# Zero-padded keys, later routing matmuls, a longer filler burst and an earlier gather in a two-stage attention and expert kernel

## The chip, the cores and the metric

The kernel runs on one core of one Trainium2 chip. The metric is the device time of one execution in microseconds (us); the median of three runs is what is compared. [...]

## What is computed

Four batches of eight-head causal attention (sequence 768, head size 64) are followed by a mixture of eight experts over the 3072 tokens. Heads 0, 2 and 6 see the whole causal triangle; the other five see the first four keys ("sinks") and a band of 64 keys.

```
scores = scale * q @ k.T            # per batch and head, causal, or band + 4 sinks
a = softmax(scores); x = a @ v      # 3072 tokens x 512
do_compute = x @ w_skip > 0         # the other tokens pass unchanged
e = argmax(x @ w_gate)              # one expert of eight for each token
out = x + prob_e * (relu(x @ w1[e]) @ w2[e])
```

## The kernel before

The order of all instructions is the order of the program text; each engine works its own instructions in that order and waits on semaphores for the others.

**Attention.** A loop over the four batches runs six slots each (`slots`, `for b in range(B)`). The heads go in pairs (0,2), (4,6), (1,3), (5,7). `trans` turns q and k of a pair on PE: 24 small transposes, of which 12 write the first head to PSUM partitions 0 to 63 and the second to 64 to 127. ACT copies the q half to the tile qT, DVE the k half to kT, so that a pair of heads shares one 128-partition tile. `retr` computes scores of a full head in three chunks (two of 1024 PSUM columns, one of 640): it writes the mask with `ident` times `tri`, adds keys times queries, and ACT takes the exponential. `strm` does a banded head in one go of 768 columns: the mask by `ident`, then six blocks, each split into two output halves of 64 keys. Both read only the 64 partitions of their own head (`r`), so these matmuls use 64 of the array's 128 rows. `sinks` does the four sink keys of the five banded heads with a 128-row, 20-column stationary operand. `outp` multiplies attention by values for a block of 128 queries of the batch before, `xt` transposes the result, `gates` computes the expert logits. PSUM holds two score buffers (`sp`) and two transposition buffers (`tp`, shared by `trans`, `xt` and routing).

**Loads.** q, k and v are converted to 16 bits by DMAs that POOL issues; `dma_step(b)` at a batch's end issues v of the next batch, q and k of the one after it, and one expert's weights. All go through one queue in order.

**Routing.** `route` is a generator, advanced by `go_on` once in each slot of the last batch and of the tail; it runs for half of the tokens at a time. PE's matmuls `rps` (ranks) and `tbp` (the slot table) stand between DVE steps. The second half runs behind the attention with bursts of `fills` between the steps: matmuls of `ident` with a zero tile, whose result is not used.

**Experts.** `gather` fetches the tokens of an expert, `xin` casts them on DVE, transposes them on PE and copies them on ACT; `up_` and `down` are the two matmul layers. For expert e the order is up_(e+1), xin(e+2), down(e).

## Time and profile before

| | us |
|---|---|
| median of 3 runs | 278.56 (278.28 to 280.26) |
| the profiled execution | 276.57 |
| its span, first to last instruction | 274.7 |
| PE busy, share of the span | 85% |
| DVE, ACT, POOL busy | 42%, 33%, 27% |
| mean granted PE clock | 0.70 |

The time of the profiled execution is 1.9 us above its span: that lies around the program. Times in the rows count from the first instruction. By place in the program: the first scores start at 9.15, the batches' first scores at 9.15, 35.29, 74.57 and 116.46; the attention outputs of the last batch run to 174.97 (the tail), the second half of the routing to 186.39, the experts to the end. PEclk is 0.50 over nearly all of the attention and 1.00 over the experts.

### The profile page before, as it was taken

What the parts mean: (1) busy time and instruction counts of PE and PEld (TensorE: products, weight loads), DVE (VectorE), ACT (ScalarE), POOL (GpSimd) and SP (SyncE); (2) the same over time, 40 slices, a digit from 0 to 9 for tenths busy, and PEclk for the clock granted to TensorE, in tenths of its full rate; (3) what the DMA queues carried; (4) which work ended last, traced back from release to release, by engine and by line L of the source; (5) the groups of instructions that cost most, each with busy time, mean ns of one, the idle gap of its engine ahead of it and who ended that gap; (6) DMA issues with size and microseconds to landing.
All of it is one profiled execution on the core that took longest, in us unless ns stands there. A gap on an engine that the chain in (4) does not pass through costs nothing.

```text
span 274.7 us, 5076 instructions
## 1 busy us (share of the span) xinstructions
PE 234.1 (85%) x2158; PEld 140.4 (51%) x2158; DVE 115.6 (42%) x282; ACT 90.9 (33%) x125; POOL 72.9 (27%) x86
## 2 busy tenths in 40 slices
PE   7799989999999999799999579792889888898930
PEld 2445545555555556455566457341666545564610
DVE  1734444244433335423458752572243334534420
ACT  2666554523254432354343134200332223122100
POOL 8652830000530000420000000006862525523540
PEclk9755575555555555755558955599599999999985
DMA  5999999999399971299511123103899999994110
GB/s 75 174 166 161 72 184 222 220 227 224 58 158 221 227 152 59 63 157 223 114 41 50 68 79 115 41 0 119 185 181 246 209 297 212 210 256 161 66 57 8
DMA packets 53137, 39.54 MB, mean 144 GB/s; under 512 B 27945, under 2 KB 44329, under 8 KB 53104
## 3 DMA queue, kind: packets, MB, share of 16 engines
q0 software_dynamic: 49648, 32.82, 79.6%
q1 hardware_dynamic: 3456, 6.29, 6.5%
q8 instruction: 19, 0.31, 0.4%
q14 instruction: 14, 0.11, 0.1%
HBM read 56.66 MB, written 10.49 MB: 244 GB/s over the span
## 4 chain that ended last, share of the span: by engine, by line
PE 69%; DVE 8%; DMA 8%; ACT 5%; issue 4%; POOL 3%; POOLq 0%; DVEq 0%; ACTq 0%
PE sps L303 10%; PE myp L654 9%; PE mhp L639 6%; DMA xg<-out_dram,idg 6%; PE sps L315 5%; PE av L359 4%; PE tps L390 4%; PE tps L265 4%; PE sps L319 3%; PE sps L300 3%; PE av L369 3%; ACT qT L274 2%; ACT atr L306 2%; PE sps L331 2%; PE sps L323 2%
## 5 line engine op out<-in xcount | busy, mean ns | idle before, releaser
L306 ACT ACTIVATE atr<-sps 128x1024 f16<-128x1024 f32 (+1 forms) x36 | 32.6, 916 | 44.2 <-PE sps L303 44.2
L601 POOL DMA_INDIRECT xg<-out_dram,idg x16 | 16.4, 1026 | 79.6 <-DVE gs L592 68.0
L303 PE MATMUL sps<-qT,kT 64*128 64x512 f16 (+3 forms) x96 | 31.6, 453 | 3.2 <-DVE kT L276 3.2
L105 POOL DMA_DIRECT2D va<-in_v_dram x8 | 11.3, 1424 | 74.3 <-PE tps L265 35.7
L639 PE MATMUL mhp<-mxT,w1t 128*128 128x256 f16 x256 | 30.6, 281 | 0.0
L654 PE MATMUL myp<-w2t,ht 128*128 128x512 f16 x128 | 28.8, 379 | 0.0
L639 PEld LDWEIGHTS <-w1t 128*128 128x128 f16 x256 | 25.8, 101 | 4.9
L276 DVE COPY kT<-tps 128x768 f16<-128x768 f16 x16 | 15.3, 955 | 27.2 <-PE tps L265 27.2
L374 DVE RECIPROCAL rec<-av 128x8 f32<-128x8 f32 x18 | 3.7, 208 | 52.9 <-PE av L371 52.9
L325 ACT ACTIVATE ats<-sps 128x768 f16<-128x768 f32 x20 | 16.2, 810 | 27.2 <-PE sps L323 27.2
L656 DVE SCALAR_TENSOR_TENSOR xg<-myp,gs,xg 128x512 f32<-128x512 f32 x16 | 12.0, 751 | 23.1 <-PE myp L654 22.2
L658 POOL DMA_INDIRECT out_dram<-xg,idx x16 | 15.9, 992 | 21.0 <-DMA w2t<-in_moe_w_dram 4.3
L645 ACT ACTIVATE ht<-mhp 128x512 f16<-128x512 f32 x16 | 9.6, 597 | 33.6 <-issue 21.8
L643 DVE TENSOR_SCALAR ht<-mhp 128x512 f16<-128x512 f32 x16 | 11.1, 692 | 19.4 <-PE mhp L639 19.4
L654 PEld LDWEIGHTS <-ht 128*128 128x128 f16 x128 | 12.3, 98 | 13.5
L628 ACT COPY mxT<-mtp 128x512 f16<-128x512 f16 x16 | 8.8, 588 | 28.0 <-PE mtp L626 28.0
L390 PE MATMUL tps<-ident,x 128*128 128x128 f16 x96 | 13.7, 293 | 4.8 <-ACT qT L274 3.7
L319 PEld LDWEIGHTS <-kT 64*64 64x64 f16 x120 | 11.6, 155 | 12.1 <-issue 11.5
L626 PE MATMUL mtp<-ident,mx 128*128 128x128 f16 x64 | 6.6, 238 | 12.8 <-DVE mx L623 12.8
L251 PE MATMUL sps<-fill,ident 128*128 128x512 f16 x52 | 15.5, 458 | 1.7 <-DVE ident L133 1.7
L323 PE MATMUL sps<-qT,kT 64*64 64x64 f16 (+2 forms) x140 | 16.3, 283 | 0.0
L319 PE MATMUL sps<-qT,kT 64*64 64x128 f16 x120 | 16.2, 300 | 0.0
(141 smaller groups left out, 389.8 us busy)
## 6 DMA issues: line engine op xcount, KB each, us to landing
w1t<-in_moe_w_dram POOLq DMA_DIRECT2D x8, 1024.0 KB, 16.8
w2t<-in_moe_w_dram POOLq DMA_DIRECT2D x8, 1024.0 KB, 20.4
out_dram<-x SPq DMA_DIRECT2D x24, 256.0 KB, 2.4
va<-in_v_dram POOLq DMA_DIRECT2D x8, 384.0 KB, 8.6
qin<-in_q_dram POOLq DMA_DIRECT2D x3, 768.0 KB, 15.1
kin<-in_k_dram POOLq DMA_DIRECT2D x3, 768.0 KB, 18.1
qin<-in_q_dram POOLq DMA_DIRECT2D x2, 192.0 KB, 4.9
kin<-in_k_dram POOLq DMA_DIRECT2D x2, 192.0 KB, 5.8
```

Source lines behind the costliest of these rows:

```text
L251: nc.tensor.matmul(ps[:, :512], ident, fill, start=True, stop=True)
L276: nc.vector.tensor_copy(o, i_)
L303: nc.tensor.matmul(ps[:, x:x + n], kT[b, pr][r, j * P:(j + 1) * P], qT[b, pr][r, q0:q0 + n], start=False, stop=True, skip_group_check=True)
L306: nc.scalar.activation(at[b, h][:, o:o + w], ps[:, :w], ACT.Exp, scale=SCALE)
L319: nc.tensor.matmul(ps[:D, c:c + P], kt[r, c:c + D], qt[r, c:c + P], start=False, stop=True, skip_group_check=True)
L323: nc.tensor.matmul(ps[D:, x:y], kt[r, c + D:c + P], qt[r, x:y], start=False, stop=True, skip_group_check=True)
L325: nc.scalar.activation(a, ps[:, :S], ACT.Exp, scale=SCALE)
L390: nc.tensor.matmul(ps[:, s], xs[g][:, s * P:(s + 1) * P], ident, is_transpose=True, start=(s == 0), stop=(s == DS - 1))
L601: nc.gpsimd.indirect_dma_start(out=xg[e, t], out_offset=None, in_=out[:, :], in_offset=bass.IndirectOffsetOnAxis(ap=idg[:, sl:sl + 1], axi ...
L639: nc.tensor.matmul(hp[:, u], w1t[:, s, f * P:(f + 1) * P], xT[:, s], start=(s == 0 and u == 0), stop=(s == DS - 1 and u == 1))
L654: nc.tensor.matmul(yp, hts[e][:, f, t * P:(t + 1) * P], w2t[:, f], start=(f == 0), stop=(f == FS - 1))
L658: sc = nc.gpsimd.indirect_dma_start(out=out[:, :], out_offset=bass.IndirectOffsetOnAxis(ap=idx[:, sl:sl + 1], axis=0), in_=xg[e, t], in_of ...
```

## The change

Every head gets a key tile of its own, `kz`, with 128 partitions: the head's keys in its own 64, zeros in the other 64. The zeros are written once, before the first batch. `trans` copies the two halves of the transposed keys apart: DVE both of them for the pairs 0 and 2, DVE the first and ACT the second for the pairs 1 and 3. `retr` and `strm` multiply all 128 partitions of `kz` by all 128 of qT. In `route`, a step ends behind the `rps` matmuls instead of behind the DVE work after them, and all twelve `tbp` matmuls come one step after the DVE work that feeds the second six. The first filler burst has 14 matmuls instead of 10, and 6 more follow the first transposes. Four experts' gathers instead of three are issued ahead of the fifth expert's weights, and xin(e+2) moves between the two token tiles of down(e).

```diff
+    kz = {h: ac.tile([P, S], FP16, name=f"kz{h}") for pr in PAIRS for h in pr}
+    for pr in PAIRS:
+        nc.vector.memset(kz[pr[0]][D:], 0.0)
+        nc.vector.memset(kz[pr[1]][:D], 0.0)
...
     def trans(b, pr):
-        for name, src, dst in (("qT", q_in, qT), ("kT", k_in, kT)):
+        for name, src in (("qT", q_in), ("kT", k_in)):
...
-            t = qtp.tile([P, S], FP16, tag=name, name=name)
-            dst[b, pr] = t
-            o = t.rearrange("c (p n) -> c p n", n=NT)
             i_ = ps.rearrange("c n p -> c p n")
             if name == "qT":
-                nc.scalar.copy(o, i_)
-            else:
-                nc.vector.tensor_copy(o, i_)
...
+                t = qtp.tile([P, S], FP16, tag=name, name=name)
+                qT[b, pr] = t
+                nc.scalar.copy(t.rearrange("c (p n) -> c p n", n=NT), i_)
+                continue
+            for i, h in enumerate(PAIRS[pr]):
+                r = slice(i * D, (i + 1) * D)
+                o = kz[h][r].rearrange("c (p n) -> c p n", n=NT)
+                if i and pr % 2:
+                    nc.scalar.copy(o, i_[r])
+                else:
+                    nc.vector.tensor_copy(o, i_[r])
...
     def retr(b, pr, i, c):
-            nc.tensor.matmul(ps[:, x:x + n], kT[b, pr][r, j * P:(j + 1) * P],
-                             qT[b, pr][r, q0:q0 + n], start=False, stop=True,
+            nc.tensor.matmul(ps[:, x:x + n], kz[h][:, j * P:(j + 1) * P],
+                             qT[b, pr][:, q0:q0 + n], start=False, stop=True,
...
     def strm(b, pr, i):
-            nc.tensor.matmul(ps[:D, c:c + P], kt[r, c:c + D], qt[r, c:c + P],
+            nc.tensor.matmul(ps[:D, c:c + P], kt[:, c:c + D], qt[:, c:c + P],
-                nc.tensor.matmul(ps[D:, x:y], kt[r, c + D:c + P], qt[r, x:y],
+                nc.tensor.matmul(ps[D:, x:y], kt[:, c + D:c + P], qt[:, x:y],
...
     def route(c0, n):
+        yield
 
         sm = mk("sm", [P, n])
...
-        yield
         rk = mk("rk", sh)
...
-            for i in range(h0, h0 + NT):
-                nc.tensor.matmul(tb, ol[:, i], mv[:, i], start=(i == 0), stop=(i == n - 1))
             yield
+            if h0:
+                for i in range(n):
+                    nc.tensor.matmul(tb, ol[:, i], mv[:, i], start=(i == 0),
+                                     stop=(i == n - 1))
...
-    fills(10)
+    fills(14)
     trans(0, 0)
+    fills(6)
...
-        for e in range(3):
+        for e in range(4):
             gather(e)
         load_w(NW, wp2)
-        for e in range(3, 5):
+        for e in range(4, 6):
...
         def down(e):
             for t in range(T2):
+                if t and e + 2 < E:
+                    xin(e + 2)
```

On DVE, behind the first batch's mask constants, the key copies of the pairs 1 and 2 stand so before (skq is the sink keys' tile, vraw a constant):

```order
L276 COPY kT<-tps 128x768
L280 COPY skq_116<-kT 64x4
L192 MEMSET vraw 20x260
L276 COPY kT<-tps 128x768
L280 COPY skq_116<-kT 64x4 x2
```

and so now:

```order
L286 COPY kz_110<-tps 64x768
L289 COPY skq_132<-kz_110 64x4
L197 MEMSET vraw 20x260
L286 COPY kz_112<-tps 64x768
L289 COPY skq_132<-kz_112 64x4
L286 COPY kz_113<-tps 64x768
L289 COPY skq_132<-kz_113 64x4
```

Pair 2 has a second copy of the same length on DVE; the second head of pair 1 is absent here because ACT copies it, between a qT copy and the next exponential.

On DVE in the expert stage, the casts of xin(2) (mx) and the updates of down(0) (xg) with the last relus (ht) stand so before:

```order
L643 TENSOR_SCALAR ht<-mhp 128x512 x4
L623 CAST mx_2800<-xg_0_2619 128x512
L623 CAST mx_2808<-xg_1_2623 128x512
L656 SCALAR_TENSOR_TENSOR xg_0_2603<-myp,gs,xg_0_2603 128x512
L656 SCALAR_TENSOR_TENSOR xg_1_2607<-myp,gs,xg_1_2607 128x512
```

and so now:

```order
L652 TENSOR_SCALAR ht<-mhp 128x512 x4
L667 SCALAR_TENSOR_TENSOR xg_0_2630<-myp,gs,xg_0_2630 128x512
L632 CAST mx_2840<-xg_0_2646 128x512
L632 CAST mx_2848<-xg_1_2650 128x512
L667 SCALAR_TENSOR_TENSOR xg_1_2634<-myp,gs,xg_1_2634 128x512
```

The casts moved from behind the last relu to behind the first update of down.

On PE the first routing's table matmuls (tbp) stood between a transposition of attention outputs (x) and the next outputs (avt, the tail's); now the tail's outputs follow the transposition, and tbp comes behind a later gate matmul.

## Rows read from the trace of the kernel before

**Rows 1.** By stretch: length, busy of PE, PEld, DVE, ACT, POOL, PEclk, DMA, GB/s

```profile
35.29:74.57 39.28, 37.93 (x386) 22.59 (x387) 16.02 (x36) 15.81 (x19) 3.71 (x4) 0.53 1.10 193
74.57:116.46 41.89, 38.98 (x403) 22.91 (x403) 16.89 (x38) 15.92 (x19) 6.22 (x7) 0.54 0.97 146
116.46:152.79 36.33, 35.27 (x386) 20.75 (x387) 18.34 (x54) 15.21 (x19) 1.91 (x3) 0.58 0.82 117
152.79:174.97 22.18, 16.00 (x215) 12.05 (x215) 10.24 (x23) 7.20 (x13) 0.00 (x0) 0.60 0.23 84
```

**Rows 2.** PE by stretch: length, busy (instructions), PEclk, DMA share, GB/s

```profile
24.91:31.04 6.13, 6.13 (x62) 0.50 0.63 47
31.04:34.31 3.27, 3.27 (x35) 0.50 2.14 137
34.31:37.70 3.39, 2.60 (x27) 1.00 2.29 156
174.97:177.67 2.70, 2.70 (x11) 0.50 0.00 0
177.67:181.00 3.33, 3.33 (x28) 1.00 0.00 0
```

**Rows 3.** Groups by form, PE, 24.91 to 31.04: busy us, mean ns

```profile
L319 PE MATMUL sps<-qT,kT 64*64 64x128 f16 x24 | 3.4, 308 | 0.0
```

**Rows 4.** Groups by form, PE, 31.04 to 34.31

```profile
L331 PE MATMUL sps<-qT,skq 128*20 128x512 f16 x3 | 1.5, 622 | 0.0
L265 PE MATMUL tps<-ident,qin 128*64 128x128 f16 x12 | 0.9, 315 | 0.0
```

**Rows 5.** Timeline of PE, third batch: start, length in us

```profile
75.54 0.39 PE L300 MATMUL sps<-tri,ident 128*128 128x128 f16 x2
...
76.83 0.27 PE L401 MATMUL av<-WgAll,xT 128*128 128x9 f16 x4
...
103.86 0.82 PE L315 MATMUL sps<-smask,ident 128*128 128x512 f16 x2
...
105.39 0.27 PE L401 MATMUL av<-WgAll,xT 128*128 128x9 f16 x4
...
107.60 0.61 PE L390 MATMUL tps<-ident,x 128*128 128x128 f16 x4
```

**Rows 6.** Timeline of PE, the same work at the upper clock

```profile
35.83 0.28 PE L300 MATMUL sps<-tri,ident 128*128 128x128 f16 x2
...
36.58 0.23 PE L359 MATMUL av<-va,atr 128*128 128x65 f16 x2
...
147.50 0.26 PE L401 MATMUL av<-WgAll,xT 128*128 128x9 f16 x4
...
149.03 0.40 PE L390 MATMUL tps<-ident,x 128*128 128x128 f16 x4
...
149.26 0.49 PE L315 MATMUL sps<-smask,ident 128*128 128x512 f16 x2
...
150.14 0.98 PE L331 MATMUL sps<-qT,skq 128*20 128x512 f16 x6
```

**Rows 7.** The tile kin, load issued at 33.9: instructions, time to landing

```profile
L100 POOL DMA_DIRECT2D kin<-in_k_dram x1: 923/923/923, 33.9 to 33.9; - x1
...
DMA to landing us min/median/max: 24.4/24.4/24.4
```

**Rows 8.** Groups by form, all: busy us, mean ns, idle before and releaser

```profile
L251 PE MATMUL sps<-fill,ident 128*128 128x512 f16 x52 | 15.5, 458 | 1.7 <-DVE ident L133 1.7
...
L276 DVE COPY kT<-tps 128x768 f16<-128x768 f16 x16 | 15.3, 955 | 27.2 <-PE tps L265 27.2
```

**Rows 9.** Timeline of PE around the first routing

```profile
155.91 0.35 PE L481 MATMUL tbp<-mv,ol 128*128 128x64 f16 x6 [2.83 <-DVE ol L477]
...
159.56 0.50 PE L481 MATMUL tbp<-mv,ol 128*128 128x64 f16 x6 [1.65 <-DVE ol L477]
```

**Rows 10.** Timeline of PE in the expert stage

```profile
222.45 0.73 PE L626 MATMUL mtp<-ident,mx 128*128 128x128 f16 x8 [1.12 <-DVE mx L623]
```

## The prediction

> **What bounds the kernel now.** I first split the span at the batches' first scores and read each stretch's engine times and PEclk [rows 1]. PE is the busy engine: 38.98 of the third batch's 41.89 us, with DVE at 16.89 and ACT at 15.92. Those two have room; PE does not. [...]

> [...] I cut short stretches at the places where the level changes [rows 2]. From 24.91 to 31.04 PE was busy all the time, and the clock stayed at 0.50. From 31.04 to 34.31 it was again busy all the time, and right after that the clock stood at 1.00 for 3.39 us. The stretches differ in the shapes. The first is made of matmuls on a quarter of the array, 64 rows by 64 columns [rows 3], with a mask matmul ahead of each head. The second has the sink scores, 128 rows by only 20 columns, and transposes that read 128 rows [rows 4]. Twenty columns raised the clock where 64 by 64 did not, so width is not the difference; the array rows that are fed are. The fillers show the same: they feed 128 rows, and the clock rose at 177.67 behind them, although their moving operand is all zeros [rows 2]. Zeros in half of the rows should therefore count like data.

> Against this reading: the sink scores of the second batch are followed by no rise, and its stretch stays at 0.53 [rows 1]. One such group is no guarantee; what stands around it matters too.

> **What the change does, part by part.**

> *Padded keys.* The score matmuls keep their number and their columns and feed 128 rows instead of 64. By the reading above they become work of the kind that raises the clock. What the upper level is worth is read from the same work at both. A 1024-column chunk of a full head, start of its masks to the start of what follows, took 76.83 - 75.54 = 1.29 us at the lower level [rows 5] and 36.58 - 35.83 = 0.75 at the upper [rows 6]. A banded head took 105.39 - 103.86 = 1.53 [rows 5] and 150.14 - 149.26 = 0.88 [rows 6]. Gates and outputs of the fifth block took 107.60 - 105.39 = 2.21 [rows 5] and 149.03 - 147.50 = 1.53 [rows 6], a ratio of 0.69.

> A batch has six long chunks, three short ones (896 of 1280 columns with the masks, so 0.70 of a long one: 0.90 and 0.53 us) and five banded heads: 6 x 1.29 + 3 x 0.90 + 5 x 1.53 = 18.1 us now and 6 x 0.75 + 3 x 0.53 + 5 x 0.88 = 10.5 at the upper level, a gain of 7.6. PE's other work in the third batch is 38.98 - 18.1 = 20.9 us; at the ratio of the outputs it gains 31%, 6.5 us. Together 14.1 us of a batch of 41.9 if the clock stayed up. PE would then take about 28 us, above ACT and DVE with what is added to them (below), so PE stays the longest.

> I do not expect it to stay up throughout. After the rise at 34.31 it lasted 3.39 us, and PE had a pause in it: 2.60 busy [rows 2]. Such pauses are at each batch's start, where the first scores wait for the key copy. I take about 4 us of each 28 at the lower level, so 85% up, and subtract what was up already, (PEclk - 0.5) / 0.5: 8% in the third batch, 16% in the fourth [rows 1]. Third batch: 14.1 x 0.77 = 10.9. Fourth: 14.1 x 0.69 = 9.7.

> The first two batches have another limit. The keys of the third were issued at 33.9 and landed 24.4 us later [rows 7], at 58.3, behind loads that keep the queue full; a faster PE does not move that. Twelve transposes and a copy of 0.96 [rows 8] put the third batch's first scores at 59.8 at the earliest, against 74.57. The first two batches gain at most 14.8 us. By PE alone they would gain 14.1 x 0.79 = 11.1 in the second and, by my estimate, a third to a half of that in the first, which has no outputs of an earlier batch and waits for the second batch's keys: 15 to 16. So the landing decides, narrowly: 14.8. Attention: 14.8 + 10.9 + 9.7 = 35.4 us.

> *Two half copies for one.* A copy runs over 768 elements per partition whichever partitions it has, so I take 0.955 us for each half [rows 8]: one more for each of 16 pairs, half of them on DVE and half on ACT. Per batch that is two each, 1.9 us on engines with 25 and 26 idle us of 41.9 and still 9 to 10 of 28. The first head's copy comes first, and its scores (0.75) run under the second one. A new wait comes with pair 3: the copy of sink keys on DVE waits for ACT's key copy, which stands behind exponentials; queued behind it on DVE is the copy of the transposed outputs, for which gates wait two slots later. I take 0. The bound, all on the path, is 16 x 0.955 = 15.3 us.

> [...]

> *Routing a step later.* The table matmuls stand in front of the tail's outputs and wait for DVE: PE idles 2.83 and 1.65 us [rows 9]. With the outputs moved ahead and the inputs a step earlier, both go: 4.5 us. What is late next is DVE, which has the same work, 18.34 of 36.33 us busy [rows 1]; bounds 0 and 4.5. In the second half, six more table matmuls come behind the last DVE work, 0.35 us for six [rows 9]: +0.4.

> *Fillers.* Ten more at 0.458 us each [rows 8] are at most 4.6 us at the start. The landing of the third batch's keys covers most of them, since the first two batches would have up to a microsecond to spare, and part of them lies under the wait for the first key copy. I take 0; the bound is 4.6.

> *Experts.* PE idles 1.12 us between up and the transposes of xin [rows 10], since the cast stands behind the last relu on DVE. Now the cast stands behind the first update of down, which itself waits for PE. The wait changes its partner, not its kind: 0, bounds -6.7 (six of them gone) and +1. The earlier gather changes the order of loads that land with time to spare: 0.

> **Sum.** 276.57 - 35.4 - 4.5 + 0.4 = 237.1 us for the profiled execution. The median of the runs is 2.0 above its own profiled one; I put the time between the two, at 238.

> **The rivals.**

> *A, the forecast.* [...] With the clock always up, 14.8 + 13.0 + 11.8 + 4.5 - 0.4 and some 3 us from a tail at the upper level: 230. Up half of the time: about 249. Own range 229 to 249.

> *B, the clock swings.* If transposes count for nothing, only the last three slots of a batch, the banded heads, are raised, and the slots with transposes fall back. Gain per batch 5 x 0.65 + 3 x 0.68 = 5.3, over three batches and the first one's heads (3.3): 19.2; 276.6 - 19.2 - 4.5 + 0.4 = 253, with the median's offset 255. For it: most slots hold 24 transposes. Against it: the 31.04 stretch is half transposes and was followed by a rise [rows 2, 4]. [...]

> *C, no change in the clock.* If what raised it were the sink scores as such, attention stays as it is: 276.6 - 4.5 + 0.4 + 2 for fillers, about 275, within 1%.

> *D, slower.* As C, and the half copies hold the transposition buffers so long that PE waits: +15.3, about 290. It decides once the waits of PE for kz and tps grow by more than 4.5 + 2.8 us. Against it: the idle time of DVE and ACT.

> **How the numbers follow.** A 0.70, B 0.19, C 0.06, D 0.05. Time 238, A's. The range reaches from A's lower end over B: 229 to 256. Faster by over 1% (about what a measurement tells from no change) is A, B and a little of C: 0.90; same 0.05; slower 0.05.

> **What would show it.** PEclk of the batches above 0.85; a long chunk at about 0.75 us in any batch; third batch's first scores near 60, held by the landing of kin; no PE idle ahead of tbp in the first routing; the pause ahead of xin still near 1.1. I am wrong if score stretches stay at 0.50 with 128 rows fed, if ACT or DVE ends PE's waits for most of a batch, or if loads of v hold the third and fourth batch.

## The result and the profile after

The changed kernel takes 241.12 us (median of four runs, 238.51 to 242.65) against 279.04 for the kernel before (four runs, 278.28 to 280.26). The ratio is 0.861 with a 95% interval of 0.852 to 0.869: faster by 14%. The profiled execution took 238.51 us, with a span of 236.6 and a mean granted clock of 0.90. Runs of one program differed by the clock that they were granted (of 32 runs of the kernel before beside the experiments below, four took 260 to 264 us at a mean clock of 0.77, a gain of 8% against those, and the others 273 to 281), so every time below is a median with its range.

PE is TensorE, and PEclk is the clock that it was granted, in parts of full speed. It was 0.50 from 98.33 to 111.26 us in the kernel before and 1.00 from 60.54 to 114.94 us in the changed one; these are the lower and the upper level. The granted clock of the changed kernel, in 40 slices of the span (tenths of full speed):

```profile
PEclk9998988999999999999955579659999999999975
```

It is up through the attention, low in the tail (slices 21 to 23), low once more at the start of the experts (slices 26 and 27), and up over the rest of them. By stretch, to be set beside [rows 1]; the columns are length, busy time of PE, PEld, DVE, ACT and POOL, PEclk, DMA share and GB/s:

```profile
9.33:31.81 22.48, 15.49 (x222) 9.86 (x220) 15.37 (x43) 16.90 (x21) 11.15 (x18) 0.92 1.66 149
31.81:60.54 28.73, 24.35 (x386) 16.88 (x387) 17.90 (x38) 17.20 (x21) 6.10 (x7) 0.94 1.41 217
60.54:89.00 28.46, 23.40 (x402) 16.56 (x403) 18.88 (x40) 17.31 (x21) 6.22 (x7) 1.00 1.47 219
89.00:114.94 25.94, 22.83 (x389) 16.19 (x390) 19.36 (x52) 16.57 (x21) 1.91 (x3) 1.00 1.43 217
114.94:134.74 19.80, 15.36 (x215) 11.61 (x213) 10.91 (x28) 7.20 (x13) 0.00 (x0) 0.60 0.28 102
134.74:147.73 12.99, 12.25 (x68) 5.25 (x65) 8.61 (x34) 0.28 (x1) 0.00 (x0) 0.82 0.00 0
147.73:236.60 88.87, 64.13 (x449) 42.16 (x449) 29.49 (x52) 18.34 (x32) 39.61 (x40) 0.90 0.79 171
```

The third batch went from 41.89 to 28.46 us with the same number of instructions on PE, whose busy time fell from 38.98 to 23.40. DVE and ACT have two more copies each, and take no longer than PE. The same work as in [rows 5], on PE in the third batch (start, length in us):

```profile
79.84 0.50 PE L321 MATMUL sps<-smask,ident 128*128 128x512 f16 x2
...
80.73 0.26 PE L407 MATMUL av<-WgAll,xT 128*128 128x9 f16 x4
...
82.26 0.40 PE L396 MATMUL tps<-ident,x 128*128 128x128 f16 x4
```

A banded head takes 80.73 - 79.84 = 0.89 us, gates and outputs 82.26 - 80.73 = 1.53: the lengths that [rows 6] had at the upper clock. PE's waits from the second batch to the tail (us, times, longest), before and then after:

```profile
PE tps L390 <- ACT qT L274: 3.7, 10, 0.6
PE sps L303 <- DVE kT L276: 2.4, 3, 1.2
...
PE tps L396 <- ACT qT L278: 8.5, 10, 1.0
PE sps L310 <- DVE kz L286: 4.6, 6, 1.6
```

PE now waits longer for the engines that clear its buffers: 13.1 us instead of 6.1.

### The profile page after: what moved, and what is told of

Read it like the earlier page. It is cut to its first block, busy times and chain, and to the rows that moved or that the text cites. A ratio compares the mean times of both kernels' runs of the same rounds, so it can differ in the third digit from the quotient of the medians.

```text
span 236.6 us, 5118 instructions
## 1 busy us (share of the span) xinstructions
PE 185.5 (78%) x2168; PEld 121.8 (51%) x2168; DVE 125.8 (53%) x298; ACT 96.1 (41%) x133; POOL 73.3 (31%) x86
## 2 busy tenths in 40 slices
DMA packets 53137, 39.54 MB, mean 167 GB/s; under 512 B 27945, under 2 KB 44329, under 8 KB 53104
## 4 chain that ended last, share of the span: by engine, by line
PE 55%; DVE 15%; DMA 13%; ACT 6%; issue 5%; POOL 2%; DVEq 0%; POOLq 0%; ACTq 0%
PE mhp L648 10%; PE myp L665 9%; DMA out_dram<-xg,idx 7%; PE sps L256 7%; DVE kz L286 4%; DMA vraw<-in_v_dram 4%; PE sps L310 4%; PE av L365 3%; PE tps L396 3%; PE av L375 3%; ACT qT L278 2%; PE sps L321 2%; DVE x L382 2%; PE mtp L635 2%; PE sps L325 2%
## 5 line engine op out<-in xcount | busy, mean ns | idle before, releaser
L665 PE MATMUL myp<-w2t,ht 128*128 128x512 f16 x128 | 29.8, 379 | 0.0
L286 DVE COPY kz<-tps 64x768 f16<-64x768 f16 x24 | 22.8, 951 | 9.6 <-PE tps L270 9.1
L105 POOL DMA_DIRECT2D va<-in_v_dram x8 | 11.3, 1423 | 47.9 <-PE av L377 22.6
L310 PE MATMUL sps<-qT,kz 128*128 128x512 f16 (+3 forms) x96 | 20.5, 320 | 4.6 <-DVE kz L286 4.6
L652 DVE TENSOR_SCALAR ht<-mhp 128x512 f16<-128x512 f32 x16 | 11.1, 691 | 20.9 <-PE mhp L648 19.8
L331 ACT ACTIVATE ats<-sps 128x768 f16<-128x768 f32 x20 | 16.2, 809 | 10.7 <-PE sps L329 10.1
L396 PE MATMUL tps<-ident,x 128*128 128x128 f16 x96 | 10.7, 241 | 12.4 <-ACT qT L278 8.5
L256 PE MATMUL sps<-fill,ident 128*128 128x512 f16 x62 | 18.9, 471 | 1.7 <-DVE ident L133 1.7
L278 ACT COPY qT<-tps 128x768 f16<-128x768 f16 x16 | 12.7, 794 | 8.3 <-PE tps L270 8.1
L307 PE MATMUL sps<-tri,ident 128*128 128x128 f16 x72 | 10.3, 227 | 5.0 <-ACT atr L313 5.0
L396 PEld LDWEIGHTS <-x 128*128 128x128 f16 x96 | 6.9, 105 | 13.9 <-issue 8.3
```

Of the source, the lines that this page charges most:

```text
L256: nc.tensor.matmul(ps[:, :512], ident, fill, start=True, stop=True)
L278: nc.scalar.copy(t.rearrange("c (p n) -> c p n", n=NT), i_)
L286: nc.vector.tensor_copy(o, i_[r])
L310: nc.tensor.matmul(ps[:, x:x + n], kz[h][:, j * P:(j + 1) * P], qT[b, pr][:, q0:q0 + n], start=False, stop=True, skip_group_check=True)
L331: nc.scalar.activation(a, ps[:, :S], ACT.Exp, scale=SCALE)
L396: nc.tensor.matmul(ps[:, s], xs[g][:, s * P:(s + 1) * P], ident, is_transpose=True, start=(s == 0), stop=(s == DS - 1))
```

## The experiments

The table gives the stretches of each profiled execution: from first scores to first scores for the batches, then to the end of the last gate matmul, of the last tbp, and of the span. The median over the runs of each kernel stands last.

| kernel | batch 1 | batch 2 | batch 3 | batch 4 and tail | 2nd routing | experts | median us (range) |
|---|---|---|---|---|---|---|---|
| before | 26.1 | 39.3 | 41.9 | 58.7 | 9.3 | 90.3 | 279.0 (278.3 to 280.3) |
| after | 22.5 | 28.7 | 28.5 | 45.7 | 11.0 | 90.9 | 241.1 (238.5 to 242.7) |
| half_rows | 26.2 | 39.5 | 40.8 | 56.3 | 11.0 | 90.7 | 275.4 (266.4 to 277.8) |
| full_only | 24.2 | 29.4 | 28.4 | 47.6 | 10.7 | 91.1 | 242.0 (239.6 to 244.2) |
| band_only | 26.2 | 37.6 | 38.2 | 53.9 | 11.3 | 91.0 | 270.6 (269.9 to 271.3) |
| pad_only | 23.0 | 29.3 | 28.5 | 50.9 | 10.1 | 91.5 | 245.6 (243.2 to 247.4) |
| seam | 21.6 | 28.5 | 26.4 | 45.3 | 11.2 | 88.8 | 232.9 (229.7 to 234.1) |
| six | 22.6 | 24.3 | 24.7 | 44.9 | 8.2 | 83.6 | 220.4 (218.7 to 222.6) |
| six_tail | 22.0 | 24.3 | 24.5 | 43.6 | 8.2 | 84.5 | 219.1 (218.5 to 221.1) |

The kernel before, run again beside them, took 278.0 us (with half_rows, full_only, band_only and pad_only), 279.3 (with fill_trans, vsk_late, vsk_loads and xin_early), 276.6 (with xt_first, seam and six) and 276.5 (with six_tail). The changed kernel was not run again beside them; its 241.1 is from its own four runs. The kept trace is of the longest run for vsk_late and xin_early, and of the shortest for the changed kernel and six.

**half_rows: is it the array rows?** All edits stay, and only the score matmuls go back to 64 rows:

```diff
+        r = slice(i * D, (i + 1) * D)
-            nc.tensor.matmul(ps[:, x:x + n], kz[h][:, j * P:(j + 1) * P],
-                             qT[b, pr][:, q0:q0 + n], start=False, stop=True,
+            nc.tensor.matmul(ps[:, x:x + n], kz[h][r, j * P:(j + 1) * P],
+                             qT[b, pr][r, q0:q0 + n], start=False, stop=True,
```

and in the same way in `strm`.

> The changed kernel with its padded key tiles, its half copies and all other edits, but the score matmuls read only the head's own 64 partitions again; the result is the same. Theory (the number of array rows fed by the scores decides the clock): PEclk of the batches falls back to 0.53 to 0.60, a long chunk takes about 1.29 us in the third batch, and the time is within 4 us of the kernel before, 275 to 283. Rival (the copies in halves, the order of the edits or the fillers brought the gain): the time stays near 241. Rival D priced alone: if the half copies cost on the path, the time is above 279 by up to 15.

Measured: 275.43 us (266.41 to 277.75; the kernel before beside it, 264.02 to 279.63). Its second and third batches by stretch, columns as above:

```profile
35.80:75.34 39.54, 37.06 (x387) 21.75 (x387) 17.90 (x38) 17.43 (x21) 2.72 (x3) 0.57 1.02 187
75.34:116.16 40.82, 37.44 (x403) 22.53 (x403) 18.87 (x40) 17.49 (x21) 6.22 (x7) 0.58 1.00 149
```

DVE and ACT do what they do in the changed kernel, and PE has the same instructions with the same columns; the clock is at 0.57 and the batches are as long as before. So the array rows that the scores feed make the gain, and the half copies cost nothing where PE is slow: except for the second routing, no stretch is longer than before by more than 0.4 us. PE was busy 37.06 of 39.54 us there, a larger share than in the changed kernel (24.35 of 28.73), with a clock of 0.57 against 0.94: a PE that was hardly ever idle stayed low.

**full_only and band_only: which heads?** Each keeps the padding of one kind of head and sends the other back to its 64 rows, by the edit above in `strm` alone (full_only) or in `retr` alone (band_only).

> The changed kernel, but only the full heads multiply all 128 partitions; the banded heads read their own 64. Theory: the clock is up in the first four slots of a batch, where the full heads stand, and falls in the last two or three, where banded heads follow one another. Worked out from the prices of the prediction, a batch gains 6 x 0.54 + 3 x 0.37 = 4.4 us on chunks and about 60% of 6.5 on other work, 8.3 in all; over three batches and a third of one, 27 us less what was up already: 252 to 260. Rival (one kind of head is enough to hold the clock): 243 or less. Rival (the clock needs both kinds all the time): 270 or more.

> The changed kernel, but only the banded heads multiply all 128 partitions; the full heads read their own 64. Theory: the clock is up in the last three slots of a batch and low in the first three. A batch gains 5 x 0.65 = 3.3 us on banded heads and about 45% of 6.5 on other work, 6.2 in all; over three batches and a third of one, 20 us: 256 to 264. Rival (one kind of head is enough): 243 or less. Rival (both are needed): 270 or more.

Measured: 242.01 us (239.59 to 244.20) with the full heads alone, no different from both, and 270.59 (269.88 to 271.31) with the banded heads alone, inside the range of the kernel before (264.02 to 279.63). My theory put the two at 252 to 260 and 256 to 264, as parts that add up. They don't: the full heads' padding is nearly all of it. What is missing from the theory stands in full_only. Its last banded head and its sink scores in the first and the third batch on PE (start, length), then the last two banded heads of the first batch, the last two slots' heads, gates and outputs in the third, and the whole third batch (columns as above):

```profile
28.11 0.82 PE L322 MATMUL sps<-smask,ident 128*128 128x512 f16 x2
...
29.64 1.77 PE L338 MATMUL sps<-qT,skq 128*20 128x512 f16 x6
...
85.17 0.49 PE L322 MATMUL sps<-smask,ident 128*128 128x512 f16 x2
...
86.05 0.98 PE L338 MATMUL sps<-qT,skq 128*20 128x512 f16 x6
```

```profile
26.99:28.11 1.12, 1.12 (x19) 0.69 (x15) 1.02 (x9) 0.81 (x1) 0.17 (x1) 0.75 0.33 20
28.11:31.35 3.24, 3.24 (x25) 1.45 (x23) 2.63 (x5) 1.62 (x2) 3.24 (x3) 0.50 0.67 45
...
79.08:86.97 7.89, 7.89 (x136) 5.18 (x134) 5.47 (x14) 4.15 (x6) 0.00 (x0) 1.00 1.21 229
...
63.23:91.67 28.44, 23.39 (x403) 16.55 (x403) 18.89 (x40) 17.30 (x21) 6.22 (x7) 1.00 1.43 222
```

The head with 64 rows took 29.64 - 28.11 = 1.53 us in the first batch, entered at 0.50, and 86.05 - 85.17 = 0.88 in the third, entered at 1.00; 0.88 is about what it takes with 128 rows too (0.89 above). The third batch's stretch from 79.08 has its like in the kernel before, with the same matmuls in the same order:

```profile
98.33:111.26 12.93, 12.93 (x134) 7.71 (x134) 4.95 (x13) 3.94 (x5) 0.00 (x0) 0.50 0.33 88
```

PE never paused in either, and the same instructions stayed at 0.50 where PE entered them at 0.50, and at 1.00 where it entered at 1.00: there the level holds itself. It does not hold everywhere. In the first batch of full_only the first three banded heads ran at 1.00, and the level fell in the fourth (26.99 to 28.11), after a pause of 1.32 us ahead of the third; these heads have no gates or outputs between them. In the changed kernel, with 128 rows, the same heads kept it behind the same pause:

```profile
25.53:29.18 3.65, 3.65 (x53) 2.02 (x52) 2.76 (x14) 3.08 (x4) 1.67 (x2) 1.00 0.73 32
```

So the banded heads' padding is worth something there: full_only's first batch took 24.2 us instead of 22.5. Band_only shows the full heads' side: at 64 rows they lose the level again in its second and third batches:

```profile
36.10:73.67 37.57, 35.27 (x387) 20.48 (x387) 17.89 (x38) 17.45 (x21) 2.55 (x2) 0.61 1.04 194
73.67:111.83 38.16, 34.78 (x402) 20.92 (x403) 18.87 (x40) 17.48 (x21) 6.21 (x7) 0.64 1.09 160
```

That the level holds itself is my reading of these kernels; a run that raises the clock by other means ahead of the same 64-row work was not made.

**pad_only: what do the other edits add?** The kernel before with padded keys, and routing, fillers, gather order and expert inputs as they were (the diff of the changed kernel without its parts on `route`, `fills`, `gather` and `xin`).

> The kernel before with padded keys alone: routing, fillers, gather order and expert inputs are those of before. Theory: nearly all of the gain is the padding's; the waits of PE for tbp in the tail come back (2 to 4.5 us), the second routing loses its extra 1.6 us, so 240 to 246. Rival (the other edits carry part of the gain, for instance because the fillers start the clock): 250 or more.

Measured: 245.63 us (243.22 to 247.42), 4.5 above the changed kernel's median. In the table nearly all of it lies in the fourth batch and the tail, 50.9 against 45.7. Of these 5.1 us, 1.7 are the fourth batch, 27.67 instead of 25.94, with pad_only's clock at 0.88 instead of 1.00, and 3.4 are the tail, 23.21 instead of 19.80:

```profile
89.60:117.27 27.67, 25.33 (x388) 17.57 (x388) 19.72 (x55) 16.61 (x21) 1.92 (x3) 0.88 1.32 206
117.27:140.48 23.21, 16.57 (x215) 12.36 (x213) 10.57 (x25) 7.21 (x13) 0.00 (x0) 0.58 0.21 80
```

In the tail the waits for the table matmuls are back (PE, start, length, idle before):

```profile
120.73 0.49 PE L487 MATMUL tbp<-mv,ol 128*128 128x64 f16 x6 [3.30 <-DVE ol L483]
...
124.91 0.50 PE L487 MATMUL tbp<-mv,ol 128*128 128x64 f16 x6 [1.63 <-DVE ol L483]
```

3.30 + 1.63 = 4.9 us, a little more than the 2.83 and 1.65 of [rows 9], since PE comes to the first one sooner. The fillers and the earlier expert inputs show in no stretch by more than 0.9 us.

**fill_trans: do transposes count?** In the second routing, 512 zero columns by `ident` become four transposes of zeros:

```diff
-    fills(6)
+    tfills(6)
     for _ in route(HALF, HALF):
-        fills(6)
+        tfills(6)
...
+        for i in range(4 * n):
+            nc.tensor.matmul(ps[:, (i % 4) * P:(i % 4 + 1) * P],
+                             fill[:, (i % 4) * P:(i % 4 + 1) * P], ident,
+                             is_transpose=True, start=(i % 4 == 0), stop=(i % 4 == 3))
```

> The changed kernel, in which each filler of the second routing (512 zero columns by ident) is replaced by four transposes of a 128 x 128 zero tile, so that 128 rows and as many columns are fed; the first fillers of the program stay as they are. Theory (transposes count like other work that feeds 128 rows): the clock, at 0.50 at the end of the tail, rises during the second routing, at about the same distance from its start as with fillers (4.8 us), and the time stays within 2 us of 241. Rival B's rule (they count for nothing): the clock stays at 0.50 through the second routing and comes up only within the experts' matmuls; 30 fillers' worth of columns at the lower level and a later rise make it 5 to 9 us slower.

Measured: 241.83 us (two runs, 241.66 and 242.01). PE had nothing but these transposes between the tail's end and the routing's matmuls. By group from 138.6 to 149.3 (busy us, mean ns, idle before), and by stretch:

```profile
L262 PE MATMUL spt<-ident,fill 128*128 128x128 f16 x148 | 10.6, 242 | 0.0
```

```profile
138.62:142.32 3.70, 3.70 (x38) 3.70 (x36) 3.00 (x14) 0.28 (x1) 0.00 (x0) 0.50 0.00 0
142.32:149.24 6.92, 6.92 (x138) 6.92 (x137) 4.23 (x11) 0.00 (x0) 0.00 (x0) 1.00 0.01 2
```

The clock rose 142.32 - 138.62 = 3.70 us after the tail's last gate matmul had ended; behind fillers, in the changed kernel, it rose 139.52 - 134.74 = 4.78 us after it. So these transposes, which feed 128 rows, raised the clock as the fillers do, and rival B has no ground.

**vsk_late and vsk_loads: what ended the first two batches?** The chain of the changed kernel that ended last (start, us, what) shows DVE's sink products, which wait for a small load, ahead of the second batch's key copies:

```profile
18.06 10.19 DMA vraw<-in_v_dram
...
28.36 2.52 DVE vsk L225 x4
30.89 0.87 DVE kz L286
```

vsk_late moves them behind those copies (`consts_4` has the products, taken out of `consts_3`); vsk_loads also issues the first expert's weights behind the third batch's queries and keys:

```diff
+            if b == 0 and i == 5:
+                consts_4()
...
         load_v(1)
-        load_w(0)
...
             load_qk(b + 2, False)
+        if b == 0:
+            load_w(0)
```

> The changed kernel, with the four products of the sink values (vsk) computed one slot later, behind the key copies of the second batch instead of ahead of them. Theory: the second batch's first scores come 1.5 to 2.5 us earlier (31.8 to about 29.7), but the third batch's do not, since the landing of its keys at 57.9 decides there: 241 within 1 us. Rival (PE's chain decides the first two batches): the third batch starts 1.5 to 2.5 us earlier too, 239.

> As the last one, and the first expert's weights (2 MB) are loaded behind the third batch's queries and keys instead of ahead of them. Theory: those keys land by 50 instead of 57.9, the third batch's first scores come 1.5 to 3 us earlier than 60.5, and the time falls to 238 to 239.5. Rival (the landing didn't decide): no more gain than the last one has.

Measured: 239.31 us (238.94 to 243.52) and 241.74 (238.26 to 243.56); with such ranges neither differs from the changed kernel by its time, so the 238 to 239.5 expected of vsk_loads did not come, and the rows decide. In vsk_late the second batch's scores began at 28.84 instead of 31.81, and the third's at 61.31, because (PE, start, length, idle before):

```profile
59.41 0.85 PE L272 MATMUL tps<-ident,kin 128*64 128x128 f16 x12 [3.30 <-DMA kin<-in_k_dram]
```

In this run the 3 us came back as a wait for the third batch's keys, as expected; the other three runs (238.94 to 239.46) have no trace. In vsk_loads that wait is gone, but the third batch began at 60.23 all the same: its second batch took 29.4 us of PE and DVE work (28.7 in the changed kernel), and the mean clock of this run was 0.882 against 0.903. The landing is one of two limits that lie within 2 us of each other.

**xin_early: is the expert pause due to the cast's place?** The casts of xin(e+2) go on DVE ahead of up(e+1); the transposes stay:

```diff
         for e in range(E):
+            if e + 2 < E:
+                cast(e + 2)
             if e + 1 < E:
                 up_(e + 1)
```

> The changed kernel, with the casts of xin(e+2) issued on DVE ahead of the matmuls of up(e+1), while the transposes stay between the two halves of down(e). Theory (the cast's place behind an update that itself waits for PE is all of PE's pause there): the pauses of 1.2 to 1.4 us ahead of mtp go for six experts, the experts' stretch shortens by 6.5 to 7.5 us, and the time is about 234. Rival (something else, ACT or the transposition buffers, holds the transposes): the pause stays over 0.6 us and the gain is under 3 us.

Measured: 236.99 us (235.52 to 239.14), where 234 was expected. In the changed kernel the pause was still there, ahead of each xin (PE, start, length, idle before):

```profile
168.20 0.73 PE L635 MATMUL mtp<-ident,mx 128*128 128x128 f16 x8 [1.18 <-DVE mx L632]
...
177.26 0.72 PE L635 MATMUL mtp<-ident,mx 128*128 128x128 f16 x8 [1.38 <-DVE mx L632]
```

In xin_early it is gone, and an expert takes 179.96 - 172.56 = 7.40 us of PE instead of 177.26 - 168.20 = 9.06:

```profile
172.56 0.61 PE L643 MATMUL mtp<-ident,mx 128*128 128x128 f16 x8
...
179.96 0.61 PE L643 MATMUL mtp<-ident,mx 128*128 128x128 f16 x8
```

The theory was right on the wait and too high on the gain: of the 6 x 1.66 = 10 us that six experts at that pace would save, PE saves 8.4 from the first transposes to its last matmul (73.6 and 65.3), and about 5 reach the end (from the first transposes to the end of the span 84.86 and 79.80). POOL is next: it issues the scatters of results only behind the last weights, one in 1.29 us. The last scatter of the changed kernel and the last two of xin_early (start, length, idle before):

```profile
226.63 0.98 POOL L669 DMA_INDIRECT out_dram<-xg,idx  x1 [0.75 <-DVE cmx L690]
```

```profile
227.25 0.99 POOL L677 DMA_INDIRECT out_dram<-xg,idx  x1 [0.30 <-issue]
228.54 0.98 POOL L677 DMA_INDIRECT out_dram<-xg,idx  x1 [0.30 <-issue]
```

In the changed kernel the last one followed PE's last work (225.40) by 1.2 us; in xin_early PE ended at 222.82 and the scatters ran on for 5.7 us, back to back.

**xt_first: are PE's waits for qT worth their length?** The transposition of the outputs (xt) moves ahead of `outp` in each slot.

> The changed kernel, with the transposition of the attention outputs (xt) issued on PE ahead of the next outputs instead of behind the key transposes of the same slot, so that it doesn't wait for the transposition buffer that ACT's copy of qT frees. The trace of the changed kernel has 8.5 us of such waits in ten places over three batches. Theory (PE is still what the second to fourth batches wait for, so its waits count in full): 5 to 8 us less, 233 to 236. Rival (ACT and DVE are by now as near to being the bound, and the wait comes back at kz or at the exponentials): less than 2 us, 239 to 241.

Measured: 240.22 us (238.16 to 242.32): the rival's time, but only in part by its mechanism. The waits for qT are gone, those for kz are nearly what they were (4.3 us), and PE stands still once for a load, which neither theory named (start, length, idle before):

```profile
59.33 0.85 PE L270 MATMUL tps<-ident,kin 128*64 128x128 f16 x12 [4.49 <-DMA kin<-in_k_dram]
```

**seam: why does the clock fall at all?** The first pair of the third and fourth batches is turned two slots early, with a fourth qT buffer; the sink products and the weights stand later:

```diff
-            ((X(2, 1), X(3, 0)), ()),
-            ((X(3, 1), lambda: sinks(b)), (T(0, b + 1),) if b + 1 < B else ()),
+            ((X(2, 1), X(3, 0)), (T(0, b + 1),) if 0 < b < B - 1 else ()),
+            ((X(3, 1), lambda: sinks(b)), (T(0, 1),) if b == 0 else ()),
...
-        if b + 1 < NW:
-            load_w(b + 1)
+        for e in ((0,), (1,), (2, 3), range(4, NW))[b]:
+            load_w(e)
```

> The changed kernel, with the first pair of the third and fourth batches turned two slots ahead of its first scores instead of right ahead of them (a fourth qT buffer for it), the sink products a slot later, and the weights issued behind queries and keys. The clock's falls in the runs of the changed kernel and of the variants stand at the batches' seams, where PE waits for the key copies and carries few matmuls. Theory (those pauses are what drops the clock): no fall at the third and fourth batches' starts, granted clock 0.90 or more in every run, and 3 to 5 us less than the changed kernel's median, 236 to 238. Rival (the falls come from elsewhere in the batch): falls remain, 239 to 242.

Measured: 232.92 us (229.73 to 234.06), better than either theory had it; 2 us of it lie in the experts' stretch, which no theory named. The mean granted clocks of its four runs are 0.897 to 0.911 (theory: 0.90 or more, which two of them miss narrowly), against 0.875 to 0.903 for the changed kernel. PE's wait for key copies from the second batch to the tail fell from the 4.6 us above to

```profile
PE sps L311 <- DVE kz L287: 1.1, 2, 0.8
```

and the clock stayed at 1.00 over the third and fourth batches. In the traces of fill_trans, vsk_late and xin_early it falls at the third or fourth batch's start (in vsk_late at 59.09, in the wait of 3.30 us above, back at 69.33; the twelve key transposes behind that wait took 0.85 us, against 0.53 in the changed kernel), so each of those starts is a place where it can be lost. Seam moves three things at once, so which of them keeps the level up is not shown; nor is that all of its gain, for its third batch is 2.1 us shorter than the changed kernel's in its trace (26.4 against 28.5), with the clock at 1.00 in both.

**six and six_tail: together.** Six has the edits of seam, xt_first and xin_early, and 4 fillers ahead of rps and 14 ahead of tbp instead of 12 and 24. Six_tail also has 15 fillers in the tail, two or three ahead of each transposition:

```diff
+        for _ in range((2, 3, 2, 2, 2, 2, 2, 0)[i]):
+            nc.tensor.matmul(av[:, 0], ident, fill, start=True, stop=True,
+                             skip_group_check=True)
```

> The edits of the last two and of xin_early in one kernel, and fewer fillers in the second routing: 4 ahead of rps instead of 12 and 14 ahead of tbp instead of 24. Theory (the parts add up): 5 us from the experts' casts, 3 to 5 from the seams, 3 to 6 from xt, 2 from the fillers: 224 to 229. Rival (they share one cover, the loads' queue, which is full through the attention): 231 or more, with PE waiting for kin or va.

> As the last one, with two or three fillers on PE ahead of each transposition of the tail, 15 in all, into a PSUM bank that nothing else uses by then. Theory (the tail gained less than the clock could give because PE's waits for DVE and ACT at its start let the clock fall, and it then stays at 0.50 for the whole tail): the fillers fill those waits, the clock stays at 1.00, the tail shortens from 19.7 to 16 or 17 us and the second routing runs at the upper level: 216 to 218. Rival (the tail is held by the chain over DVE and ACT, or the fillers don't hold the clock): the tail stays at 19.7 or grows by up to 15 x 0.43 = 6.5 us: 220 to 226.

Measured: 220.43 us (218.66 to 222.58) and 219.13 (218.50 to 221.13); both beat both kernels, six beats its theory too (224 to 229), and the two do not differ. In six the order of xt, worth nothing alone, pays once the loads are out of its way. Its second batch to the tail, and then the tail of six_tail:

```profile
31.26:55.55 24.29, 22.73 (x386) 15.84 (x387) 19.93 (x41) 17.10 (x21) 2.88 (x4) 1.00 1.49 213
55.55:80.23 24.68, 23.27 (x404) 16.45 (x403) 19.13 (x40) 17.02 (x21) 6.21 (x6) 1.00 1.42 214
80.23:105.39 25.16, 22.71 (x390) 16.10 (x389) 20.29 (x53) 16.50 (x21) 6.11 (x6) 1.00 1.42 223
105.39:125.09 19.70, 16.05 (x218) 12.04 (x213) 10.84 (x27) 7.21 (x13) 0.00 (x0) 0.54 0.90 213
```

```profile
105.73:124.21 18.48, 16.28 (x231) 10.54 (x228) 10.85 (x27) 7.20 (x13) 0.00 (x0) 0.91 0.95 226
```

PE is busy for 22.73 of 24.29 us, so six is again bound by PE, now at its upper clock. The tail's fillers did hold the clock (0.91 instead of 0.54), but the tail shortened by 1.2 us, not by 3, the fillers' own time included: with the clock up, its steps wait for the chain over DVE and ACT. PE was busy 16.28 of 18.48 us there, and 0.97 + 0.22 + 0.44 + 0.39 = 2.02 us of the rest are its waits for x on DVE, x on ACT (twice) and xT on ACT.

## Why the prediction was right, point by point

The forecast was 238 us, the sum for the profiled execution 237.1; measured were 241.12 and 238.51. The profiled time is 1.4 from the sum, in part by luck: the third and fourth batches gained 3.2 us more than forecast, and both routings, the first two batches and the experts together 4.5 less. The median lies 2.6 above its own profiled run; two of the four runs had a lower mean clock (0.875 against 0.902 and 0.903). They have no trace; where the other kernels' traces lose the level in the third and fourth batches, it is at their starts.

- **Array rows raise the clock: right, and shown** by half_rows (0.57 and 0.58 in the second and third batches, 0.94 and 1.00 with 128 rows). A banded head has the length that was read from the upper clock, 0.89 against 0.88. A long chunk is shorter than the 0.75 read there [rows 6], 66.40 - 65.85 = 0.55 (PE in the changed kernel's third batch):

```profile
65.85 0.28 PE L307 MATMUL sps<-tri,ident 128*128 128x128 f16 x2
...
66.40 0.28 PE L307 MATMUL sps<-tri,ident 128*128 128x128 f16 x2
```

  Both were at the upper clock (masks of 0.28 us, as in [rows 6], against 0.39 at 0.50 in [rows 5]); the 0.75 was read from 64 rows, and half_rows has it again in the first batch (13.60 - 12.85) where the changed kernel has 13.03 - 12.47 = 0.56. So part of the padding's gain is not the clock's, and the sum had put it at nothing. But the step that all "score matmuls" have to "become work of the kind that raises the clock" asked too much: by full_only the nine chunks of the full heads are enough from the second batch on (1.00 over full_only's third), where the five banded heads keep what those raised.
- **Clock up for 85% of a batch: too low.** In the profiled run it was 1.00 over the third and fourth batches; the traces of fill_trans, vsk_late and xin_early spend 7 to 10 us of the third at 0.50. The third gained 41.89 - 28.46 = 13.4 us (10.9 forecast); the sum's own figure for a clock always up, 14.1 x 0.92 = 13.0, was near, but by two errors that cancel: PE's busy time fell by 38.98 - 23.40 = 15.6 us, and its idle time grew from 2.9 to 5.1. The fourth gained 36.33 - 25.94 = 10.4 (9.7 forecast, 11.8 for a clock always up): PE now waits for qT and kz there.
- **First two batches, 14.8 by the landing of keys: right in size (14.2), half right in cause.** In the changed kernel PE turned those keys at 57.97 without a wait, and the first scores at 60.54 waited for DVE's copies. Vsk_late shows the landing right behind that: once PE came sooner, it stood 3.30 us until 59.41. Moving both was not enough either: the two batches took 51.2 us in the changed kernel, 51.1 in vsk_loads and 50.1 in seam, and 46.9 only in six, where the waits for qT are gone too.
- **Half copies, nothing: right where PE is slow,** since half_rows has them all and is no longer than the kernel before. A half copy on DVE, 64 partitions by 768, took 0.951 us on average in the changed kernel, where the whole one, 128 by 768, took 0.955 [rows 8]; on ACT it took 0.793. At the upper clock no run separates them; PE's waits for the copies of queries and keys grew from 6.1 to 13.1 us.
- **Routing, 4.5: too high.** The tail went from 22.18 to 19.80, 2.4 us; against pad_only's tail it is 3.4. The waits ahead of tbp are gone, but what is late next, DVE and ACT with the same work, came due inside it (PE in the changed kernel's tail):

```profile
117.26 0.40 PE L396 MATMUL tps<-ident,x 128*128 128x128 f16 x4 [1.22 <-DVE x L390]
...
120.42 0.61 PE L396 MATMUL tps<-ident,x 128*128 128x128 f16 x4 [1.52 <-ACT x L388]
...
121.03 0.80 PE L489 MATMUL tbp<-mv,ol 128*128 128x64 f16 x12
```

  The clock fell at 119.04, as the second of these waits began, and the rest of the tail ran at 0.50. In six_tail the tail's mean clock was 0.91 instead of six's 0.54, and 1.2 us came back, so DVE's and ACT's chain is the larger part.
- **Second routing, +0.4: mis-sized, +1.6.** The clock rose only 4.78 us behind the tail, against 2.70 before [rows 2], so that the fillers ahead of rps ran at the lower clock and past the time at which their successor was ready. With fewer of them the stretch went from 11.0 to 8.2 us (six).
- **First fillers, nothing: right** (first two batches 52.3 us in pad_only, 51.2 after). **Experts, nothing: right** (+0.6), with the pause still at 1.2 to 1.4 us; xin_early shows that it could go, and that POOL takes half of it back.

Rival B fell with fill_trans. Rival C's clock was seen in half_rows, where the padding is undone. Rival D did not come, but its sign nearly did: PE's waits for qT and kz grew by 13.1 - 6.1 = 7.0 us over three batches, where the prediction let it decide from 4.5 + 2.8 = 7.3. They lie within batches that are 10 to 13 us shorter each.

## What to carry to other kernels

Where PE is busy almost all the time and PEclk still stands at 0.50, look at how many array rows its matmuls feed; here zeros in the unused rows cost no time on PE (a banded head took 0.89 us with them and 0.88 without, both at 1.00) and bought the upper clock (1.00 in the third batch, against 0.58 in half_rows). Find by variants which part loses the clock (here the full heads), and then guard the places where PE pauses: the same work that held the upper level for 7.89 us in full_only did not win it back in 12.93 us in the kernel before. When PE gets faster, look at once for the load, the copy and the queue that were just hidden behind it, since several limits may lie close together: here two lay within 2 us of one another, and moving one alone gave nothing that the time tells (239.31 us, 238.94 to 243.52, in vsk_late, against 241.12, 238.51 to 242.65).
